# A softmax-attention block and two feed-forward layers on one core: later w_in products, and a table that shifts 32 operations in a list scheduler

## The chip, the cores and the metric

The kernel runs on one core of one Trainium2 chip. Five engines of the core share the work: TensorE (PE in the profile, with PEld for its weight loads), VectorE (DVE), ScalarE (ACT), GpSimd (POOL) and SyncE (SP), which here does nothing but issue DMAs. The metric is the device time of one execution in microseconds, of which the median over three runs is given.

## The reference, cut to what matters

Eight heads in each of four batches attend to 32 state rows, and the state rows attend back to the 512 tokens; the results go through two feed-forward layers of 2304 tokens each.

```python
scores = x @ state.T / 8;   a  = softmax(scores);   xread = a @ state       # per head: 512 x 32 scores
scores2 = state @ x.T / 8;  a2 = softmax(scores2);  sread = a2 @ x
x = concat(xread, sread)                       # (2304 tokens, 512)
h = x @ w_in                                   # moe: 512 -> 2048
g = where(h >= 1, h, where(h <= -1, 0, (h + 1) ** 2 / 4))
x = g @ w_out                                  # 2048 -> 512
a, b = x @ w_a, x @ w_b                        # moe2: 512 -> 1536
out = (a * b) @ w_out2                         # 1536 -> 512
```

Everything is float32. The weights arrive as 64-bit words and are turned to float32 on the chip.

## The kernel before, in words

**Precision by parts.** A large product is made in three passes. Each operand is split into a high part (ACT copies it into the fp32r type, `hi_of`, line 346) and a low part (DVE subtracts the high part from the operand, `tt`, line 356); PE then adds up high x high, high x low and low x high (`mms`, line 371). So before nearly every PE step there stands one ACT instruction and one DVE instruction.

**Phase one** is the attention with the first layer's first product, `h`. The tokens of a batch are one block `j` (0 to 3), the hidden features 16 groups `f`; one step `t = 16 j + f` makes the unit `h_mm(j, f)`: six matmuls of 512 columns into one of four PSUM banks. Then `gate` (lines 779, 788 and 793) applies the activation: ACT, then ACT or POOL, then DVE, which frees the bank, then a store to the scratch tensor `g_d`.

What `h_mm(j, f)` reads was folded beforehand. The product `xread @ w_in` is never made from `xread`: `w_state(j, n)` (line 660, called by `phase_one`) multiplies the state of block j with four groups of `w_in` (f = 4n to 4n + 3) into a PSUM pair named `upper`; ACT and DVE split that into the buffer `wsum[n]`; then `h_mm` multiplies `wsum` with the softmax `att`. There is one `wsum[n]`, so `w_state(j + 1, n)` may only overwrite it when `h_mm(j, 4n + 3)` is done, and must be done before `h_mm(j + 1, 4n)`. For the first groups of block 0 it is made in pieces of 128, 128 and 256 columns.

Beside it run: `w_in(f, 2)`, which loads two groups of weights and turns them to float32 in three steps, `copy` (ACT, DVE or POOL: line 421 or 423), `byte` (ACT, line 346) and `join` (DVE, line 434); the scores and softmax of the next block (`b_qk`, line 526, `b_soft`, lines 543 to 569); the state's own attention of each block (`s_soft`, lines 695 to 726, `s_tr`, line 743, `s_read`, line 758), through a PSUM pair named `lower`; and the conversion of `w_out` (`conv`, then `v_early`, `v_upper`, `v_rest`: sums of quarters in line 904, on DVE or POOL, and splits in 356).

**The later phases** are `g @ w_out` (`b_steps`) in three chunks of tokens, and the second layer (`ab_run`, `o_run`). They are made with seven block products in place of eight, whose sums and differences of quarters DVE makes (line 904), each followed by a split (ACT 346, DVE 356) that the next twelve matmuls wait for. `late` puts the second layer's weights (`w_sums`, `w_put`) into the end of `b_steps`.

**What sets the order.** Nothing is issued where it is written. Each operation is recorded by `Flow.op` with its engines, an assumed cost, what it reads and writes. `Flow.order` then lists all 2344 operations: for each it works out a latest start `late` backwards from the end, and steps through assumed time, giving each engine the ready operation with the smallest `late`. PE operations keep the order in which they were recorded, save those marked `loose`, which may be put in wherever PE would wait. Where an operation may run on several engines, the listing picks one. The result is a fixed order of instructions on each engine and in SP's DMA queue; on the chip each engine runs its list in order and waits at semaphores.

Of the kernel before, what the change touches and what calls it, by code (L numbers as in the profile page):

```python
# [14 lines left out]
AX = mybir.AxisListType  # L15
PSUM = bass.MemoryType.PSUM
DRAM = bass.MemoryType.DRAM


class Flow:  # L20
# [13 lines left out]
    def __init__(self):  # L34
        self.ops = []
        self.last = {}
        self.readers = {}
        self.loose = set()
        self.gate = None
        self.hold = None  # L40
        self.row = None
        self.rush = 0.0
        self.port = set()
        self.hurry = {}

    def op(self, engs, emit, rd=(), wr=(), size=0, loose=False, port=False):
        i = len(self.ops)
# [37 lines left out]
    def order(self):  # L85
# [24 lines left out]
        for i in range(n - 1, -1, -1):  # L110
# [5 lines left out]
            if i in ideal:  # L116
                late[i] = min(late[i], ideal[i])
        late = [x - self.hurry[i] for i, x in enumerate(late)]
        free = dict.fromkeys(self.LAT, 0.0)
        ready = {e: [] for e in free}  # L120
        left = [len(d) for _, _, d, _ in ops]
# [13 lines left out]
        for _ in range(n):  # L135
# [39 lines left out]
                fin[i] = wire + self.DMA_LAT  # L175
            for s in after[i]:
                left[s] -= 1
                when[s] = max(when[s], free[e] if (e,) == (*ops[s][0],) and not ops[i][3] else fin[i])
                if not left[s]:
                    offer(s)  # L180
            self.ops[i] = (*ops[i][:4], e)
# [5 lines left out]
def attention_then_two_mlps(  # L187
# [458 lines left out]
    def w_state(*args):  # L646
        for f in w_steps(*args):
            f()

    def w_steps(b, n, f0=0, f1=4):  # L650
# [4 lines left out]
        def emit(e):  # L655
            for j in range(4):
# [14 lines left out]
                emit,  # L671
                regs(*st, win.sub(2048 * n + 512 * f0, 512 * (f1 - f0))),
                [bank(b) for b in ab],
                loose=b == 0 and n > 0,
            )
        ]
        for q in [range(2)] if WIDE and cols == 4 * P else [range(1), range(1, 2)]:
# [654 lines left out]
    def phase_one():  # L1332
# [39 lines left out]
        for b, (soft, tr, read, after) in enumerate(TIMES):  # L1372
            PLAN.setdefault(soft, []).append((s_soft, b))
            PLAN.setdefault(tr, []).append((s_tr, b))
            PLAN.setdefault(read, []).append((s_read, b))
            if b < 3:
                if b:
                    PLAN.setdefault(16 * b - 5, []).append((st_load, b + 1))
                PLAN[soft].append((lambda b: (a_load(2 * b), a_load(2 * b + 1)), b + 1))
                PLAN.setdefault(after, []).extend([(b_qk, b + 1), (b_soft, b + 1)])  # L1380
        nv = 0
        for t in range(4 * F1):
            j, f = divmod(t, F1)
# [4 lines left out]
            h_mm(j, f, (1,) if t < HALVES else range(2))  # L1388
            for g in (v1, v2)[t] if t < 2 else ():
                g()  # L1390
            if j < 3 and f % 4 == 3:
                w_state(j + 1, f // 4)
            for what, b in PLAN.get(t, ()):
                flow.hold = units[HOLD] if b < 1 else None
                flow.rush = RUSH[b]
# [97 lines left out]
    for t0 in pairs:  # L1493
        o_run(t0, t0 == pairs[-1])

    order = flow.order()
    with tc.manual_schedule():
        nc.vector.memset(half, 0.5)
# [79 lines left out]
```

## Time and profile before

| | |
|---|---|
| median of 3 runs | 720.42 us (719.61 to 723.85) |
| the profiled execution | 719.44 us, its span 717.3 us |
| PE busy | 699.2 us, 97% |
| DVE, ACT, POOL busy | 559.3, 424.8, 97.3 us |

The span is the time between the first and the last instruction; 2.1 us lie around it. A PE matmul counts as busy also where it runs at half the clock; the granted clock is in the windows' column PEclk (1.00 is 2.4 GHz).

### The profile page before, as it was taken

To read this page: it belongs to the slowest core of one execution; us is meant where nothing else is said; L and a number is where in the kernel's file an instruction comes from. 1 tells how busy PE (TensorE), PEld (TensorE's weight loads), DVE (VectorE), ACT (ScalarE), POOL (GpSimd) and SP (SyncE) were. 2 spreads that over 40 slices of the span, in tenths; PEclk is the share of its full clock that TensorE was granted. 3 is DMA by queue.
4 is the path that set the end of the run, shared out by engine and by line. 5 is a ranking of instruction groups with operands and counts; after the bars stand their busy time and mean duration, and the time that the engine had idled before them with its cause. 6 is when DMAs were issued, how large, how long until landed. Compare 5 with 4: busy or idle time off the path is not lost.

```text
span 717.3 us, 12235 instructions
## 1 busy us (share of the span) xinstructions
PE 699.2 (97%) x4818; PEld 655.4 (91%) x4818; DVE 559.3 (78%) x701; ACT 424.8 (59%) x625; POOL 97.3 (14%) x72
## 2 busy tenths in 40 slices
PE   7799999999999999999999999999999999999997
PEld 5456667989899999999999999999999999999997
DVE  6888879988998687899899786655636798987760
ACT  4787989797544446666566675655425535544440
POOL 3346555573100000000000000000000000000000
PEclk9999999999999999999999999999999999999999
DMA  9867967497466157143425767454541248454201
GB/s 346 357 214 245 357 236 272 149 349 250 147 200 242 35 162 219 50 141 138 133 99 203 226 203 243 157 167 135 183 163 42 87 150 279 127 188 136 87 30 44
DMA packets 75449, 128.92 MB, mean 180 GB/s; under 512 B 5632, under 2 KB 51200, under 8 KB 75392
## 3 DMA queue, kind: packets, MB, share of 16 engines
q1 hardware_dynamic: 75392, 128.15, 53.1%
q8 instruction: 37, 0.61, 0.4%
q14 instruction: 20, 0.16, 0.1%
HBM read 84.87 MB, written 43.25 MB: 179 GB/s over the span
## 4 chain that ended last, share of the span: by engine, by line
PE 82%; DVE 7%; DMA 5%; ACT 2%; issue 2%; POOL 1%; SPq 0%; DVEq 0%; POOLq 0%; ACTq 0%
PE bank L371 76%; DMA f<-in_w_dram 2%; PE bank L829 2%; DVE rh L356 2%; DMA p_d<-f 1%; DMA f<-p_d 1%; PE upper L660 1%; DVE r L356 1%; PE lower L758 1%; PE bank L853 1%; ACT f L346 1%; DVE fs L434 1%; DVE fs L549 1%; DVE fs L793 1%; ACT rh L346 0%
## 5 line engine op out<-in xcount | busy, mean ns | idle before, releaser
L371 PE MATMUL bank<-rh,r 128*128 128x352 f32 (+2 forms) x1398 | 223.5, 316 | 2.6 <-DVE rh L356 2.1
L371 PEld LDWEIGHTS bank<-rh,r 128*128 128x128 f32 x1398 | 215.8, 189 | 4.6 <-DVE rh L356 3.0
L371 PE MATMUL bank<-r,r 128*128 128x368 f32 (+1 forms) x960 | 156.1, 315 | 0.0
L346 ACT ACTIVATE f<-bank 128x368 f32<-128x368 f32 (+3 forms) x183 | 82.4, 453 | 119.3 <-PE bank L371 118.3
L371 PEld LDWEIGHTS bank<-r,r 128*128 128x128 f32 x960 | 147.9, 188 | 0.0
L346 ACT ACTIVATE rh<-f 128x736 fp32r<-128x736 f32 (+5 forms) x120 | 100.7, 846 | 77.7 <-PE bank L371 61.3
L356 DVE TENSOR_TENSOR rh<-f,rh 128x736 fp32r<-128x736 f32 (+5 forms) x120 | 120.2, 1014 | 26.1 <-ACT rh L346 25.6
L356 DVE TENSOR_TENSOR f<-bank,f 128x368 f32<-128x368 f32 (+2 forms) x168 | 85.6, 516 | 69.0 <-PE bank L371 64.0
L371 PE MATMUL bank<-r 128*128 128x512 f32 (+1 forms) x582 | 122.1, 362 | 2.8 <-ACT r L346 1.1
L371 PEld LDWEIGHTS bank<-r 128*128 128x128 f32 x582 | 95.5, 191 | 28.5 <-issue 5.1
L346 ACT ACTIVATE r<-f 128x768 fp32r<-128x768 f32 (+6 forms) x85 | 80.0, 952 | 40.8 <-PE bank L371 17.6
L356 DVE TENSOR_TENSOR r<-f,r 128x768 fp32r<-128x768 f32 (+6 forms) x85 | 91.9, 1090 | 15.7 <-ACT r L346 15.6
L371 PE MATMUL bank<-rh 128*128 128x352 f32 (+2 forms) x564 | 93.3, 318 | 0.5 <-DVE f L356 0.5
L904 DVE TENSOR_TENSOR f<-f 128x256 f32<-128x256 f32 (+7 forms) x108 | 85.8, 811 | 6.3 <-DMA f<-p_d 5.2
L371 PEld LDWEIGHTS bank<-rh 128*128 128x128 f32 x564 | 88.4, 189 | 1.4 <-issue 0.7
L371 PE MATMUL bank<-r,rh 128*128 128x368 f32 (+1 forms) x480 | 80.3, 315 | 0.0
L371 PEld LDWEIGHTS bank<-r,rh 128*128 128x128 f32 x480 | 74.3, 188 | 0.0
L346 ACT ACTIVATE f<-f 128x1024 fp8e5<-128x1024 f32 (+1 forms) x43 | 47.8, 1120 | 2.2 <-POOL f L423 2.0
L421 ACT ACTIVATE f<-f 128x512 fp8e5<-128x512 fp8e5 (+1 forms) x29 | 29.5, 1018 | 24.5 <-DMA f<-in_w_dram 18.4
L434 DVE SCALAR_TENSOR_TENSOR f<-f 128x1024 uint32<-128x1024 uint32 (+1 forms) x34 | 34.9, 1027 | 5.9 <-ACT f L346 5.8
L779 ACT ACTIVATE f<-bank,half 128x512 f32<-128x512 f32 x40 | 27.1, 686 | 8.1 <-PE bank L371 4.4
L793 DVE SCALAR_TENSOR_TENSOR f<-f,bank 128x512 f32<-128x512 f32 x40 | 26.3, 675 | 6.6 <-POOL f L788 4.0
(65 smaller groups left out, 425.9 us busy)
## 6 DMA issues: line engine op xcount, KB each, us to landing
f<-in_w_dram SPq DMA_DIRECT2D x25, 1024.0 KB, 6.2
f<-g_d SPq DMA_DIRECT2D x36, 368.0 KB, 5.5
f<-p_d SPq DMA_DIRECT2D x17, 768.0 KB, 5.0
g_d<-f SPq DMA_DIRECT2D x40, 256.0 KB, 4.3
f<-in_w_dram SPq DMA_DIRECT2D x18, 512.0 KB, 3.9
p_d<-f SPq DMA_DIRECT2D x48, 184.0 KB, 2.1
g_d<-fs SPq DMA_DIRECT2D x28, 256.0 KB, 3.6
f<-g_d SPq DMA_DIRECT2D x16, 352.0 KB, 4.5
```

What stands on the lines that cost most here:

```text
L346: lambda e: nc.scalar.activation(dst(), src(), func, **{k: (v() if callable(v) else v) for k, v in kws.items()}),
L356: op({"DVE": t_tt(n)}, lambda e: nc.vector.tensor_tensor(dst(), a(), b(), alu), rd, wr, port=port)
L371: nc.tensor.matmul(o, w, x, start=first and k == 0, stop=last and k == n - 1, skip_group_check=onto)
L421: nc.scalar.activation(to(), of(), AF.Copy, saturate=False)
L434: lambda e: nc.vector.scalar_tensor_tensor(out(U32), words_of(1, U32)(), 5, z(U32), ALU.logical_shift_right, ALU.bitwise_or),
L549: op({"DVE": 1.25}, lambda e: nc.vector.transpose(t1(), wide["lower"]), both, regs(t1))
L660: nc.tensor.matmul(banks[ab[q]][o : o + NS, :cols].rearrange("p (f x) -> p f x", x=P), st[q]()[64 * h : 64 * h + 64, NS * j : NS * j + NS] ...
L758: nc.tensor.matmul(banks[4][64 * e2 : 64 * e2 + 64, o : o + NS], xn()[:, c * 256 + p * 128 + e2 * 64 : c * 256 + p * 128 + (e2 + 1) * 64], ...
L779: lambda e: nc.scalar.activation(g(), h(), AF.Relu, bias=half[:, 0:1], scale=0.5),
L793: lambda e: nc.vector.scalar_tensor_tensor(g(), g(), 1.0, h(), ALU.min, ALU.max),
L829: nc.tensor.matmul(banks[b][:, P * i : P * i + P], w[:, P * c : P * c + P], xs()[:, P * c : P * c + P], start=c == 0, stop=c == 3,)
L904: lambda e: eng(e).tensor_tensor(dst(), a(), b(), alu),
```

## The change

Three things. `w_state` of blocks 1 to 3 is marked `loose` too, and called some four steps later (`AHEAD` gives, for a step t, the pair of block and n). `Flow.order` takes a table `NUDGE`: for an operation's number in the recording, an amount taken off its latest start (positive: earlier in the choice, negative: later), and for two of them an engine that it may not use. And an operation keeps the scheduler's rule for operations with one engine, as it was recorded, where the table takes an engine away.

```diff
+NUDGE = {
+    64: (119,), 65: (2433,), 72: (638,), 78: (-4.5,), 79: (20.5, "POOL"), 90: (-9.5,), 92: (658.5,), 100: (78,),
...
+    1278: (9.5,),
+}
@@ Flow.order
+        single = [len(e) == 1 for e, _, _, _ in ops]
+        for i, (x, *off) in self.nudge.items():
+            late[i] -= x
+            ops[i] = ({e: t for e, t in ops[i][0].items() if e not in off}, *ops[i][1:])
...
-                when[s] = max(when[s], free[e] if (e,) == (*ops[s][0],) and not ops[i][3] else fin[i])
+                when[s] = max(when[s], free[e] if single[s] and e in ops[s][0] and not ops[i][3] else fin[i])
@@ w_steps
-                loose=b == 0 and n > 0,
+                loose=b > 0 or n > 0,
@@ phase_one
+        AHEAD = {7: [(1, 0)], 11: [(1, 1)], 15: [(1, 2)], 19: [(1, 3)], 22: [(2, 0)], 26: [(2, 1)], 30: [(2, 2)], 34: [(2, 3)], 38: [(3, 0)], 42: [(3, 1)], 45: [(3, 2)], 47: [(3, 3)]}
...
-            if j < 3 and f % 4 == 3:
-                w_state(j + 1, f // 4)
+            for b, n in AHEAD.get(t, ()):
+                w_state(b, n)
...
+    flow.nudge = NUDGE
     order = flow.order()
```

Line numbers of the changed kernel are 14 higher in what follows (660 becomes 674).

**The order at three places.** First, PE in the first 45 us. `bank0` to `bank3` (L371) are units of `h_mm` of block 0, in the order of f from 1 on; `upper` (L660) are `w_state` products, `lower` L743 the transposes of `s_tr`, L758 `s_read`. Before:

```order
L371 MATMUL bank1_68<-r0_65 128x512 x6
L660 MATMUL upper_88<-fs_92 32x256 x8
L660 MATMUL upper_88<-fs_92 32x512 x8
L371 MATMUL bank2_69<-r0_65 128x512 x6
L371 MATMUL bank3_70<-r0_65 128x512 x6
L660 MATMUL upper_88<-fs_92 32x512 x8
L371 MATMUL bank0_67<-r0_65 128x512 x6
L743 MATMUL lower_87<-ident_64,fs_92 128x128 x4
L371 MATMUL bank1_68<-r0_65 128x512 x6
L743 MATMUL lower_87<-ident_64,fs_92 128x128 x4
```

And now:

```order
L385 MATMUL bank1_68<-r0_65 128x512 x6
L674 MATMUL upper_88<-fs_92 32x256 x8
L385 MATMUL bank2_69<-r0_65 128x512 x6
L674 MATMUL upper_88<-fs_92 32x512 x8
L385 MATMUL bank3_70<-r0_65 128x512 x6
L757 MATMUL lower_87<-ident_64,fs_92 128x128 x4
L385 MATMUL bank0_67<-r0_65 128x512 x6
L757 MATMUL lower_87<-ident_64,fs_92 128x128 x4
L674 MATMUL upper_88<-fs_92 32x512 x8
L385 MATMUL bank1_68<-r0_65 128x512 x6
L772 MATMUL lower_87<-fs_92 64x32 x32
L674 MATMUL upper_88<-fs_92 32x512 x8
```

The unit f = 2 now stands ahead of the product for f = 4 to 7; block 1's first product, which followed the unit f = 3, now comes after f = 5 (last row), and the product for f = 8 to 11, which followed f = 7, now follows f = 4.

On DVE in the same place (L434 joins weights, L423 is a `copy`, L356 `128x128` and `128x256` are the low parts that the units f = 1 and f = 2 wait for, L695 `s_soft`'s maximum) there stood:

```order
L434 SCALAR_TENSOR_TENSOR fs_92<-f0_66 128x1024
L434 SCALAR_TENSOR_TENSOR fs_92<-f0_66 128x512
L423 COPY f0_66<-f0_66 128x1024
L356 TENSOR_TENSOR r0_65<-upper_88,r0_65 128x128 x2
L695 TENSOR_REDUCE fs_92<-lower_87 128x2
L434 SCALAR_TENSOR_TENSOR fs_92<-f0_66 128x1024 x2
L356 TENSOR_TENSOR r0_65<-upper_88,r0_65 128x256 x2
```

Now:

```order
L448 SCALAR_TENSOR_TENSOR fs_92<-f0_66 128x512
L448 SCALAR_TENSOR_TENSOR fs_92<-f0_66 128x1024
L709 TENSOR_REDUCE fs_92<-lower_87 128x2
L370 TENSOR_TENSOR r0_65<-upper_88,r0_65 128x128 x2
L807 SCALAR_TENSOR_TENSOR f0_66<-f0_66,bank0_67 128x512
L715 TENSOR_SCALAR fs_92<-fs_92 128x2
L448 SCALAR_TENSOR_TENSOR fs_92<-f0_66 128x1024
L437 COPY f0_66<-f0_66 128x1024
L370 TENSOR_TENSOR r0_65<-upper_88,r0_65 128x256 x2
```

The narrow join is first, the first copy has gone to POOL (another stands in its place further down), the maximum has moved ahead, and one of the two wide joins has moved behind the 256-wide low parts.

Second, POOL at the end of phase one. L904 are sums of quarters of `w_out`, L788 squares of `gate`; the last row of before runs beside the splits of `b_steps`' second and third products.

```order
L904 TENSOR_TENSOR f0_66<-f0_66 128x4x256 x2
L788 TENSOR_TENSOR f0_66<-f0_66 128x512 x3
L904 TENSOR_TENSOR f0_66<-f0_66 128x4x256
L788 TENSOR_TENSOR f0_66<-f0_66 128x512
L904 TENSOR_TENSOR f0_66<-f0_66 128x4x256
L788 TENSOR_TENSOR f0_66<-f0_66 128x512 x5
L904 TENSOR_TENSOR f0_66<-f0_66 128x4x256 x2
```

Now:

```order
L918 TENSOR_TENSOR f0_66<-f0_66 128x4x256
L557 TENSOR_TENSOR fs_92<-fs_92 128x1024
L918 TENSOR_TENSOR f0_66<-f0_66 128x4x256
L437 COPY f0_66<-f0_66 128x1024
L918 TENSOR_TENSOR f0_66<-f0_66 128x4x256
L802 TENSOR_TENSOR f0_66<-f0_66 128x512
L918 TENSOR_TENSOR f0_66<-f0_66 128x4x256 x4
L802 TENSOR_TENSOR f0_66<-f0_66 128x512 x4
L918 TENSOR_TENSOR f0_66<-f0_66 128x4x256
L802 TENSOR_TENSOR f0_66<-f0_66 128x512 x4
```

There are eight sums on POOL in place of six (DVE has the two fewer), four of them stand in a row, and four squares follow the last one.

Third, DVE in the last chunk of `b_steps`, where `w_put` splits the second layer's first weights (`128x512` and `128x1280`) between the splits that PE waits for (`128x2x352`); L356 with `bank` adds a finished PSUM bank and frees it.

```order
L356 TENSOR_TENSOR rh_1271<-f1_1275,rh_1271 128x2x352
L356 TENSOR_TENSOR rh_1271<-f1_1275,rh_1271 128x512
L356 TENSOR_TENSOR rh_1271<-f1_1275,rh_1271 128x1280
L356 TENSOR_TENSOR rh_1271<-f1_1275,rh_1271 128x2x352 x3
L356 TENSOR_TENSOR f0_66<-bank5_1256,f0_66 128x352
L904 TENSOR_TENSOR f0_66<-f0_66 128x256
L356 TENSOR_TENSOR f0_66<-bank4_1255,f0_66 128x352
```

Now:

```order
L370 TENSOR_TENSOR rh_1274<-f1_1278,rh_1274 128x2x352
L370 TENSOR_TENSOR f0_66<-bank4_1258,f0_66 128x352
L370 TENSOR_TENSOR rh_1274<-f1_1278,rh_1274 128x512
L370 TENSOR_TENSOR f0_66<-bank5_1259,f0_66 128x352
L370 TENSOR_TENSOR rh_1274<-f1_1278,rh_1274 128x2x352 x2
L370 TENSOR_TENSOR rh_1274<-f1_1278,rh_1274 128x1280
L370 TENSOR_TENSOR rh_1274<-f1_1278,rh_1274 128x2x352
```

The 1280-wide low part stands behind two more of the splits, and the two bank additions ahead of them.

## Rows read from the trace of the kernel before

**Rows 1.** The page: span, and busy time of each engine.

```profile
span 717.3 us, 12235 instructions
PE 699.2 (97%) x4818; PEld 655.4 (91%) x4818; DVE 559.3 (78%) x701; ACT 424.8 (59%) x625; POOL 97.3 (14%) x72
```

**Rows 2.** Windows, by stage: length, busy us of each engine, clock, DMA share.

```profile
18.00:27.00 9.00, 4.41 (x51) 2.20 (x59) 8.63 (x12) 6.93 (x11) 2.53 (x2) 1.00 1.03 409
27.00:32.00 5.00, 5.00 (x27) 3.33 (x23) 4.13 (x6) 4.14 (x7) 2.12 (x3) 0.66 1.02 406
32.00:60.00 28.00, 25.94 (x238) 16.52 (x238) 24.69 (x29) 22.64 (x29) 14.68 (x11) 1.00 0.63 206
60.00:128.00 68.00, 67.05 (x590) 46.30 (x588) 56.55 (x72) 59.45 (x91) 41.68 (x32) 1.00 0.78 278
128.00:176.00 48.00, 48.00 (x302) 44.13 (x295) 42.44 (x42) 39.91 (x55) 24.74 (x14) 1.00 0.75 255
176.00:190.00 14.00, 12.49 (x73) 11.78 (x72) 13.86 (x11) 8.51 (x9) 5.38 (x2) 1.00 0.27 83
295.00:330.00 35.00, 33.94 (x209) 33.34 (x209) 32.22 (x37) 20.94 (x30) 0.00 (x0) 1.00 0.42 138
330.00:718.00 388.00, 383.47 (x2627) 382.79 (x2625) 279.93 (x386) 199.78 (x307) 0.00 (x0) 1.00 0.45 144
```

**Rows 3.** Waits of PE: for whom, us in total, times, longest.

```profile
PE upper L660 <- DVE r L356: 4.1, 3, 2.5
```

**Rows 4.** Timeline of PE, 20 to 62: start, us, tile, shape, count [idle before <-releaser].

```profile
20.64 0.45 PE L660 MATMUL upper<-fs 64*32 64x128 f32 x16 [1.33 <-DVE fs L434]
...
26.87 1.13 PE L660 MATMUL upper<-fs 64*32 64x512 f32 x16 [2.46 <-DVE r L356]
...
54.36 1.09 PE L660 MATMUL upper<-fs 64*32 64x512 f32 x16 [1.26 <-DVE r L356]
55.39 5.78 PE L371 MATMUL bank<-r 128*128 128x512 f32 x24
```

**Rows 5.** Timeline of DVE, 18 to 27.

```profile
18.75 1.83 DVE L434 SCALAR_TENSOR_TENSOR fs<-f 128x1024 uint32<-128x1024 uint32 x2 [0.33 <-ACT f L346]
20.62 1.78 DVE L423 COPY f<-f 128x1024 uint8<-128x1024 uint8 x1
...
22.69 1.21 DVE L695 TENSOR_REDUCE fs<-lower 128x2 f32<-128x1024 f32 x1
...
26.07 0.74 DVE L356 TENSOR_TENSOR r<-upper,r 128x256 fp32r<-128x256 f32 x2
```

**Rows 6.** Timeline of ACT: two byte conversions.

```profile
21.81 2.58 ACT L346 ACTIVATE f<-f 128x1024 fp8e5<-128x1024 f32 x2 [0.17 <-POOL f L423]
```

**Rows 7.** Windows: the stretch at half clock.

```profile
27.80:31.20 3.40, 3.40 (x16) 2.60 (x9) 2.53 (x3) 3.40 (x7) 0.93 (x1) 0.50 1.03 411
```

**Rows 8.** Timeline of PE, 60 to 128: the two waits.

```profile
88.45 4.37 PE L371 MATMUL bank<-r 128*128 128x512 f32 x18 [0.57 <-DVE fs L793]
...
119.39 2.06 PE L758 MATMUL lower<-fs 128*64 128x32 f32 x64 [0.38 <-ACT fs L346]
```

**Rows 9.** Timeline of DVE and POOL, 139 to 186: quarter sums, splits beside them.

```profile
139.52 1.23 DVE L904 TENSOR_TENSOR f<-f 128x1024 f32<-128x1024 f32 x1
...
176.27 5.46 POOL L904 TENSOR_TENSOR f<-f 128x1024 f32<-128x1024 f32 x2 [7.80 <-DVE r L356]
177.45 5.06 DVE L356 TENSOR_TENSOR rh<-f,rh 128x736 fp32r<-128x736 f32 x2
184.64 0.91 DVE L356 TENSOR_TENSOR rh<-f,rh 128x736 fp32r<-128x736 f32 x1
```

**Rows 10.** Timeline of DVE and PE, 294 to 330: six splits, two PE waits.

```profile
294.30 5.30 DVE L356 TENSOR_TENSOR rh<-f,rh 128x704 fp32r<-128x704 f32 x6
...
298.04 29.11 PE L371 MATMUL bank<-rh,r 128*128 128x352 f32 x179 [0.60 <-DVE rh L356]
327.61 2.65 PE L371 MATMUL bank<-rh 128*128 128x352 f32 x15 [0.46 <-DVE f L356]
```

More of the change, by code (lines that the diff above doesn't have):

```diff
@@ L17 @@
 DRAM = bass.MemoryType.DRAM
+NUDGE = {
+    64: (119,), 65: (2433,), 72: (638,), 78: (-4.5,), 79: (20.5, "POOL"), 90: (-9.5,), 92: (658.5,), 100: (78,),
+    109: (-9,), 138: (69,), 163: (-32,), 196: (-9,), 219: (-12.5,), 304: (7.5,), 328: (6, "ACT"), 1010: (33,),
+    1011: (30.5,), 1092: (10,), 1094: (-1.5,), 1096: (10,), 1103: (5.5,), 1138: (-5.5,), 1170: (10,),
+    1172: (191.5,), 1182: (-1,), 1201: (-5,), 1208: (29.5,), 1211: (27,), 1213: (10.5,), 1217: (8,), 1235: (-4.5,),
+    1278: (9.5,),
+}
 class Flow:
@@ L44, in __init__ @@
         self.hurry = {}
+        self.nudge = {}
     def op(self, engs, emit, rd=(), wr=(), size=0, loose=False, port=False):
```

## The prediction

> **What bounds the kernel now.** I read the page first: PE is busy 699.2 of 717.3 us [rows 1]. What PE has to multiply is not changed by one matmul, so only two things can be won: the time in which PE stands still, 18.1 us, and the time in which its clock is down. Next, the windows by stage, to see where that lies [rows 2]: 18 to 27 us leaves PE idle for 4.59 us, 32 to 60 for 2.06, 60 to 128 for 0.95, 176 to 190 for 1.51, 295 to 330 for 1.06. The stretch 128 to 176 leaves nothing, and the last 388 us only 4.53, of which the end of the last store is most. Of the first 18 us the lists of instructions are the same in both kernels. Last, who ends the waits: the longest is the `w_state` product into `upper`, 4.1 us in three waits for a subtraction on DVE [rows 3], and DVE is busy 8.63 of 9 us from 18 to 27 and 24.69 of 28 from 32 to 60. So up to 60 us the order of DVE's list sets the time, and PE pays for each instruction that stands ahead of the one it waits for. Behind 60 us PE itself is the bound, with four short waits in it.
>
> **Head, 18 to 32 us.** (a) The 1024-wide join waits 0.33 us for ACT and stands ahead of the 512-wide one, and a copy of 1.78 follows [rows 5] (1.83 for both joins, so by width about 1.2 and 0.6); the product for the unit f = 1 waits 1.33 us for the narrow join [rows 4]. With the narrow one first, that product can start when PE comes to it, at 20.64 - 1.33 = 19.3. The low parts that the unit f = 1 needs stood behind two joins and the copy, so at about 18.75 + 1.83 + 1.78 = 22.3; now they stand behind the two joins (from 18.4, no wait) and the maximum of 1.21, so at 18.4 + 1.83 + 1.21 = 21.4: about 0.8 earlier. (b) The 256-wide low parts for f = 2 start at 26.07 [rows 5], because ACT had two byte conversions of 2.58 us ahead of their high parts [rows 6]; these start earlier, since the copy before them now runs on POOL. On DVE there are, from 21.4, the two small low parts (0.5, from 0.74 for twice the width), a gate as wide as the narrow join (0.6), a wide join (1.2) and a copy of 1.78 or less: 25.3. (c) PE idles 2.46 us and then makes the product for f = 4 to 7 first [rows 4]. In the new order the unit f = 2 goes into that idle time: four units take 5.78 [rows 4], one 1.4. The product needs the second wide join, which now stands behind the 256-wide low parts: 25.3 + 0.74 + 1.2 = 27.2, against 26.87. So at this point PE is 1.4 - 0.3 = 1.1 us ahead; bounds 0 and 1.5.
>
> (d) From 27.8 to 31.2 the granted clock is 0.50, that is 1.2 GHz, with PE busy throughout [rows 7]: 3.4 us at half speed lose 1.7. It fell behind the stage in which PE was busy 4.41 of 9 us [rows 2], and every later window shows 1.00. Where PE does the unit f = 2 earlier, it is busier ahead of 27.8, about 5.8 of 9. The rows show one fall and no near miss, so they can't say whether that is enough. I take half, 0.85; bounds 0 and 1.7. The Trainium skill (TensorE: Matmul & The Clock Gate, section "What's actually happening") calls the slow clock the default, which activity releases; the trace agrees as far as 0.50 follows the emptiest stage, and by that rule the fuller PE keeps its clock, which would make the sum 0.85 larger.
>
> **32 to 60 us: 2.06 idle, of which 1.26 is one wait** at 54.36 for DVE [rows 2, 4]. The deferred products each take 1.09 of PE [rows 4], one ACT instruction and a subtraction of about 1.2 on DVE with them; up to the unit f = 12 there is one fewer than before. That is not work saved, it returns between 60 and 128, but there DVE has 11.4 us of slack [rows 2]. Against it stands the product for f = 8 to 11, moved from behind f = 7 to behind f = 4. It needs the join of f = 10, which on DVE follows the low part of the product made at 27.2 (1.1 on PE, a high part as long as one conversion, 1.3 [rows 6], a low part as long as a sum of that width, 1.2 [rows 9]: 30.8) and another copy: 30.8 + 1.8 or less + 1.2 = 32.5 to 33.8. PE is there after two more units and a transpose, near 32. PE's list is strict, so all units stand behind that wait; I take 1.0. Net 2.06 - 1.0 = 1.05; bounds -1.0 (DVE as late as before, and the new wait) and 2.06. Head together: 1.1 + 0.85 + 1.05 = **3.0**, between -1.0 and 5.3.
>
> **60 to 128: 0.95 idle** [rows 2]. The wait of 0.38 for ACT before `s_read` of the last block [rows 8] goes, because a unit and a product (1.4 + 1.1 us) now stand between its transposes and it. The wait of 0.57 for a gate on DVE stays: gate, transposition, gate stand as before. I take **0.4**. Above, 0.95; below, -1.7, three new waits like that one, since ACT is busy 59.45 of 68 us.
>
> **176 to 190: 1.51 idle** [rows 2]. Two splits of 736 columns take 5.06 us together beside two sums on POOL of 5.46, while one alone takes 0.91 [rows 9]: 3.2 us lost on DVE, and PE's two waits follow. Both sums now run earlier, so the splits get back to 0.9 and both waits go. But the sums run somewhere else, beside other two-operand instructions of DVE, in a stage where PE has waited for nothing yet. I take **1.0**; above 1.5, below see the first rival.
>
> **295 to 330: 1.06 idle** [rows 2]. The split at whose end PE starts at 298.04 stood behind a 1280-wide subtraction. Six of them in a row take 5.30 [rows 10], four of 704 columns, one of 512 and the widest; by width (4608 columns) these are about 0.8, 0.6 and 1.5. That one now comes two splits later, and two bank additions of about 0.5 come ahead: 0.5 less, and a small sum that also went behind gives 0.4 more. That makes 0.9, against 0.60 of idle time. The bank addition that ends the second wait (0.46 idle) now comes ahead of a split instead of behind it, 0.8 earlier. I take **0.9**; bounds 0 and 1.06. Past 330 us, little can be won (4.53, mostly the end), and the few changes there I cost at nothing; PE at 383.47 of 388 covers them, and if that cover fails they cost a wait of half a us each.
>
> **Sum.** 3.0 + 0.4 + 1.0 + 0.9 = 5.3. The profiled execution takes 719.44, 0.98 under the median of 720.42; against it 714.1, and as a median 720.4 - 5.3 = **715.1**.
>
> **Rivals.** *The sums on POOL hold DVE up (slower).* The row says that a split beside a POOL sum takes 2.5 us in place of 0.9 [rows 9]. POOL gets eight sums for six, four in one row, all ahead of 176. DVE has 48 - 42.44 = 5.56 us of slack from 128 to 176 [rows 2], and 2.46 more without its own two sums of 1.23 [rows 9]: 8.0. Into this stage come four more POOL sums. If each holds up one DVE instruction by 1.6, that is 6.4, and PE notices nothing. If each holds up two, it is 12.8, 4.8 over the slack, and the units of block 3 wait for their banks. The point is 2.0 us of delay for each sum. Together with a head at its lower bound of -1.0, nothing from 60 to 128 and the two later gains (1.5 and 0.9): -1.0 - 4.8 + 1.5 + 0.9 = -3.4, or 723.8. For it: DVE at 42.44 of 48; against: many of DVE's instructions there read PSUM. The Trainium skill (GPSIMD Engine Reference, section "Key points") says that GpSimd shares its SBUF interfaces with VectorE, with contention where DVE has two SBUF inputs; the trace agrees with 2.5 against 0.91. By that rule alone every such DVE instruction under a sum pays, as in the case with two.
>
> *The waits only change place.* DVE remains as full as it was up to 60 us, so a product that PE meets earlier waits there instead, and the clock falls again: head 0.2, nothing to 128, 1.0 and 0.9 behind: 2.1, or 718.3. This also holds if the list does on the chip what it did before, because its order rests on assumed durations (a DVE instruction beside POOL is taken there as at most doubled, and the row says 2.8 times). For it: DVE at 24.69 of 28 and the DMA share above 1.0 from 18 to 32 [rows 2], so the weights cannot come sooner.
>
> *Every wait goes and the clock stays up*: 5.3 + 0.95 + 1.5 + 1.06 = 8.8, or 711.6. For it: the lists put work of PE into each of the gaps named.
>
> **Chances.** The forecast's case (gains of 3.2 to 7.2) 0.58; every wait goes 0.16; waits change place 0.19; the slower one 0.07. One per cent is 7.2 us, about what a measurement of this kernel can tell from no change; faster by more than that needs nearly all that stands still behind 18 us, so 0.17; slower by more than 1% (over 727.6) would need a second loss of the first rival's size, 0.03; within, 0.80. The range: from 710.6, the best case with 1.0 for the spread of the runs, to 720.6, which holds the waits that change place with a loss of 2.3 more and leaves out the slower rival.
>
> **What would show it.** In the new profile: PE's `upper` products no longer lead the table of waits, and the 2.46 us before the product of f = 4 to 7 shrink to under 1; the wait moves to the product of f = 8 to 11, near 33 us. The window near 28 to 31 shows 1.00 or 0.50, which decides 1.7 us. Splits of 736 columns take 0.9 throughout 176 to 190 with PE at 14 of 14; in 128 to 176 PE stays within 0.5 of full. At 295 to 330 PE misses under 0.3. The prediction is wrong if DVE's two-operand instructions at 130 to 165 take 2.5 us in number and PE waits for gates there, or if ACT, fuller than any other engine but PE from 60 to 128, makes new waits of its own.

## The result, and the profile after

The changed kernel takes **711.81 us** (median of 4 runs, 711.13 to 711.93) against 720.36 (719.61 to 723.85) in the same comparison: a ratio of 0.987, interval 0.984 to 0.990. The gain is 8.55 us where 5.3 were forecast; it lies inside the range, but beyond the forecast's own case (3.2 to 7.2) and just beyond one per cent, which had got a chance of 0.17.

The profiled execution took 711.84 us, its span 710.1. The page, span and busy times, answering [rows 1]:

```profile
span 710.1 us, 12246 instructions
PE 697.3 (98%) x4818; PEld 653.9 (92%) x4818; DVE 556.5 (78%) x701; ACT 421.1 (59%) x622; POOL 105.3 (15%) x75
```

PE stands still for 710.1 - 697.3 = 12.8 us, where it was 18.1: 5.3 us less. The windows by stage, as in [rows 2], with one more for 190 to 295:

```profile
18.00:27.00 9.00, 6.01 (x53) 2.70 (x60) 7.91 (x14) 7.84 (x14) 4.19 (x3) 0.89 1.02 409
27.00:32.00 5.00, 4.90 (x32) 2.60 (x16) 3.58 (x3) 3.62 (x5) 1.56 (x2) 0.85 1.02 409
32.00:60.00 28.00, 27.01 (x245) 17.34 (x244) 26.76 (x34) 24.94 (x38) 13.75 (x11) 1.00 0.68 236
60.00:128.00 68.00, 67.55 (x603) 49.20 (x602) 58.13 (x70) 58.49 (x86) 48.96 (x35) 1.00 0.83 289
128.00:176.00 48.00, 48.00 (x290) 43.24 (x290) 43.76 (x41) 38.65 (x52) 30.53 (x16) 1.00 0.70 236
176.00:190.00 14.00, 14.00 (x85) 14.00 (x84) 12.98 (x12) 6.59 (x9) 0.00 (x0) 1.00 0.51 160
190.00:295.00 105.00, 104.59 (x627) 103.83 (x626) 85.16 (x97) 54.75 (x76) 0.00 (x0) 1.00 0.49 161
295.00:330.00 35.00, 35.00 (x218) 34.79 (x217) 33.08 (x38) 22.09 (x32) 0.00 (x0) 1.00 0.43 135
```

Idle time of PE by stage, before and after: 18 to 32 us 4.59 and 3.09, 32 to 60 2.06 and 0.99, 60 to 128 0.95 and 0.45, 176 to 190 1.51 and 0, 190 to 295 0 and 0.41, 295 to 330 1.06 and 0. In the table of waits, the products into `upper` no longer lead [rows 3]; units of `h_mm` that wait for their weights do:

```profile
PE bank L385 <- ACT r L360: 2.0, 3, 0.8
PE bank L385 <- DVE r L370: 1.6, 2, 0.9
...
PE upper L674 <- DVE fs L448: 0.4, 1, 0.4
```

PE's timeline shows where they are, beside [rows 4]:

```profile
18.97 0.73 PE L385 MATMUL bank<-r 128*128 128x512 f32 x2 [0.56 <-ACT r L360]
20.46 1.19 PE L385 MATMUL bank<-r 128*128 128x512 f32 x4 [0.76 <-DVE r L370]
...
23.04 0.73 PE L385 MATMUL bank<-r 128*128 128x512 f32 x2 [0.79 <-ACT r L360]
24.64 1.75 PE L385 MATMUL bank<-r 128*128 128x512 f32 x4 [0.87 <-DVE r L370]
26.32 1.96 PE L674 MATMUL upper<-fs 64*32 64x512 f32 x16
...
33.09 0.66 PE L757 MATMUL lower<-ident,fs 128*128 128x128 f32 x4 [0.99 <-ACT fs L740]
33.67 1.09 PE L674 MATMUL upper<-fs 64*32 64x512 f32 x16
```

The wait of 2.46 us ahead of the product for f = 4 to 7 is gone; the units f = 1 and f = 2 wait four times for under 0.9 us. A new wait near 33 us is there as foreseen, 0.99 us, but one step earlier, at the transposes and for ACT instead of a join on DVE. The product takes 1.96 us in place of 1.13 because the clock fell again, as in [rows 7]:

```profile
25.10:28.40 3.30, 3.30 (x21) 0.89 (x20) 3.14 (x4) 1.33 (x3) 1.35 (x1) 0.50 1.03 413
```

DVE and POOL around the sums of quarters, beside [rows 9]:

```profile
137.37 11.46 POOL L918 TENSOR_TENSOR f<-f 128x1024 f32<-128x1024 f32 x4
138.05 2.79 DVE L370 TENSOR_TENSOR r<-f,r 128x1024 fp32r<-128x1024 f32 x1
141.36 2.83 DVE L370 TENSOR_TENSOR rh<-f,rh 128x1024 fp32r<-128x1024 f32 x1
146.51 3.11 DVE L370 TENSOR_TENSOR rh<-f,rh 128x736 fp32r<-128x736 f32 x1
...
174.33 1.93 DVE L370 TENSOR_TENSOR rh<-f,rh 128x736 fp32r<-128x736 f32 x2
```

Three splits are slow beside the four sums in a row, but PE is busy 48.00 of 48 us there; the two splits of 736 columns that took 5.06 beside late sums, the ninth and tenth of their kind, now take 1.93. And PE at the third place, beside [rows 10]:

```profile
274.02 7.84 PE L385 MATMUL bank<-rh,r 128*128 128x352 f32 x47 [0.41 <-DVE rh L370]
281.71 7.83 PE L385 MATMUL bank<-rh 128*128 128x352 f32 x48
289.37 31.11 PE L385 MATMUL bank<-rh,r 128*128 128x352 f32 x192
```

Both waits of [rows 10] are gone; one of 0.41 us has come at 274.

**How far ahead, and since when.** The same matmul starts in the two traces at 16.52 and 15.24 us (first unit of `h_mm`), 142.37 and 138.24 (first of block 3), 190.60 and 184.35, 283.52 and 277.84, 299.93 and 293.24, 327.61 and 320.32, and the last at 713.72 and 706.50. The lead is 1.28, 4.13, 6.25, 5.68, 6.69, 7.29 and 7.22 us. The first 1.28 are there before the lists differ. They come from the first stretch; PE's timeline of before, and then of after:

```profile
1.36 5.06 PE L853 MATMUL bank<-ident 128*128 128x128 f32 x22 [1.36 <-POOL ident masks.py:199]
```

```profile
1.36 4.25 PE L867 MATMUL bank<-ident 128*128 128x128 f32 x22 [1.36 <-POOL ident masks.py:199]
```

The same 22 matmuls take 0.81 us less, because the clock rose from 0.50 to 1.00 earlier in that execution, at 4.58 us for 7.32. In the 14 traces of this case the first unit, up to which PE's list is the same in all, starts between 15.08 and 16.60 us. So 1.28 us of the traced gain is chance; 5.94 come behind it.

### The profile page after: what moved, and what is told of

The parts are those of the page before. It is cut to its first block, busy times and chain, and to the rows that moved or that the text cites. A ratio compares the mean times of both kernels' runs of the same rounds, so it can differ in the third digit from the quotient of the medians.

```text
span 710.1 us, 12246 instructions
## 1 busy us (share of the span) xinstructions
PE 697.3 (98%) x4818; PEld 653.9 (92%) x4818; DVE 556.5 (78%) x701; ACT 421.1 (59%) x622; POOL 105.3 (15%) x75
## 4 chain that ended last, share of the span: by engine, by line
PE 89%; DMA 4%; DVE 3%; ACT 2%; issue 1%; POOL 0%; DVEq 0%; POOLq 0%; ACTq 0%
PE bank L385 82%; PE bank L843 2%; PE upper L674 2%; DMA f<-in_w_dram 2%; DMA g_d<-fs 1%; PE lower L772 1%; DMA f<-g_d 1%; ACT f L360 1%; PE bank L867 1%; DVE f L918 1%; DVE rh L370 1%; DVE r L370 1%; DMA f<-x_d 0%; PE lower L540 0%; PE lower L757 0%
## 5 line engine op out<-in xcount | busy, mean ns | idle before, releaser
L385 PE MATMUL bank<-rh,r 128*128 128x352 f32 (+2 forms) x1398 | 222.4, 316 | 0.9 <-ACT f L360 0.5
L385 PEld LDWEIGHTS bank<-rh,r 128*128 128x128 f32 x1398 | 215.9, 189 | 1.7 <-DVE rh L370 0.7
L385 PE MATMUL bank<-r,r 128*128 128x368 f32 (+1 forms) x960 | 156.2, 315 | 0.0
L385 PEld LDWEIGHTS bank<-r,r 128*128 128x128 f32 x960 | 147.8, 188 | 0.1
L370 DVE TENSOR_TENSOR f<-bank,f 128x368 f32<-128x368 f32 (+2 forms) x168 | 85.8, 517 | 72.3 <-PE bank L385 68.0
L370 DVE TENSOR_TENSOR rh<-f,rh 128x736 fp32r<-128x736 f32 (+5 forms) x120 | 119.2, 1002 | 25.5 <-ACT rh L360 25.0
L385 PE MATMUL bank<-r 128*128 128x512 f32 (+1 forms) x582 | 121.1, 360 | 4.5 <-ACT r L360 2.0
L385 PEld LDWEIGHTS bank<-r 128*128 128x128 f32 x582 | 94.7, 190 | 30.0 <-issue 8.4
L370 DVE TENSOR_TENSOR r<-f,r 128x768 fp32r<-128x768 f32 (+6 forms) x85 | 94.3, 1122 | 15.6 <-ACT r L360 15.6
L385 PE MATMUL bank<-rh 128*128 128x352 f32 (+2 forms) x564 | 93.5, 318 | 0.1
L385 PEld LDWEIGHTS bank<-rh 128*128 128x128 f32 x564 | 88.4, 189 | 1.2 <-DVE f L370 0.6
L918 DVE TENSOR_TENSOR f<-f 128x256 f32<-128x256 f32 (+6 forms) x106 | 83.3, 804 | 6.1 <-DMA f<-p_d 5.0
L385 PE MATMUL bank<-r,rh 128*128 128x368 f32 (+1 forms) x480 | 80.3, 315 | 0.0
L385 PEld LDWEIGHTS bank<-r,rh 128*128 128x128 f32 x480 | 74.3, 188 | 0.0
```

What stands on the lines that cost most here:

```text
L370: op({"DVE": t_tt(n)}, lambda e: nc.vector.tensor_tensor(dst(), a(), b(), alu), rd, wr, port=port)
L385: nc.tensor.matmul(o, w, x, start=first and k == 0, stop=last and k == n - 1, skip_group_check=onto)
L918: lambda e: eng(e).tensor_tensor(dst(), a(), b(), alu),
```

## The experiments

**Splices.** In the first four kernels the order is a fixed list, made of the new list up to one unit and of the old one behind it, or the other way round; what runs is the same. With the list in the file, line numbers are some 130 higher (L674 becomes L801, L385 L512, L370 L497).

```diff
-    order = flow.order()
+    order = ORDER
+    for i, e in enumerate(ENGINE):
+        flow.ops[i] = (*flow.ops[i][:4], names[e])
```

*New up to the first unit of block 1 (60 us), then old.*

> The lists of the changed kernel up to the first unit of block 1 (about 60 us), those of the kernel before from there on. Theory A (each group of moves takes away the wait beside it, and the gains add up): 1.9 us faster than before, as the profiles' lead at equal work says (3.1 at that unit, less 1.3 that was there before the lists differ), so 718.5; the PE waits at 176 to 190 and 295 to 330 are there as before. Rival G (the lead of the head is given back, since DVE and ACT are nearly full behind it): under 0.5 us. Rival S (the lead is where the clock rises in that execution, not the lists): between 0 and 1.3, without a wait less in 18 to 60.

Measured: 720.00 us (before beside it 720.91), ratio 0.9991, 0.9970 to 1.0011: nothing that can be told from no change. PE's timeline at the seam:

```profile
60.40 1.96 PE L801 MATMUL upper<-fs 64*32 64x512 f32 x16 [2.08 <-DVE r L497]
62.29 5.07 PE L512 MATMUL bank<-r 128*128 128x512 f32 x18
```

PE comes to the first product of the old list early and waits 2.08 us for DVE; then the clock falls, and the product takes 1.96 us in place of 1.09, the 18 matmuls 5.07 in place of 4.37. In this trace the lead of the head is gone: less the start of the execution, the product begins as late as before.

*New up to the first unit of block 3 (about 138 us), then old.*

> The new lists up to the first unit of block 3 (about 128 us in the profile before), the old ones from there. Theory A: 2.9 us faster than before (lead 4.1 at that unit in the profiles, less 1.3), 717.5. Rival G: under 1. Rival S: as with the new lists to 60 us.

Measured: 715.02 us, ratio 0.9927, 0.9900 to 0.9955: 5.9 us are won by then, twice the 2.9 of Theory A. PE's two waits behind the late sums are still in its trace, 0.75 us each, at 181 and 184 us.

*New up to the fifth split of the third product group (about 200 us), then old.*

> The new lists up to the fifth split of the third product group (about 200 us), the old ones from there. Theory A: 4.9 us faster than before, since the 1.8 of waits at 184 and 188 go too: 715.5; PE then waits at 297 and 327 as before (1.06). Rival: the lead of the earlier part is lost where the sums on POOL hold DVE up, and this kernel is no faster than the one that is new to 128 us.

Measured: 712.60 us, ratio 0.9896, 0.9868 to 0.9924: another 2.4 us, 8.3 in all, where Theory A had 4.9; the two waits of 0.75 are gone, and those of 0.60 and 0.46 at 293 and 323 us are there as before the change. The rest of the list, with that place, brings the remaining 0.8 to the new kernel's 711.81; the forecast for it was 0.9. The two times come from different comparisons, though: by the gains, each over its own kernel before (720.91 and 720.36), it is 0.2, by the traces, less the start, 1.2.

*Old up to the first unit of block 1, then new.*

> The old lists up to the first unit of block 1, the new ones from there. Theory A: what the whole change gains less the part of the head: 8.5 - 1.9 = 6.6 by the medians, 4.1 by the profiles; so 714 to 716, with the head's waits (2.46 at 26.9, 1.26 at 54.4) as before. Rival G or S: as fast as the changed kernel within 1 us, since the head's moves bring nothing.

Measured: 718.46 us, ratio 0.9968, 0.9949 to 0.9987. Both theories missed: the whole change behind 60 us is worth only 2.5 us with the old head. PE's timeline at the seam shows the mirror image of the first splice, a wait for ACT:

```profile
63.37 1.27 PE L884 MATMUL lower<-ident,fs 128*128 128x128 f32 x8 [1.86 <-ACT fs L867]
```

So head and middle do not add up: 0.9 (not clear of nothing) for the one and 2.5 for all that follows it, but 8.6 together. In both traces PE waits at the seam for an engine whose list behind it does not have its work that early. A caution goes with all four: part of what a seam costs is the seam's own, and no run separates the two.

**The old order traced once more**, as a fixed list, nothing changed:

> The order of the kernel before, written out as a fixed list: nothing is changed in what runs. The question is what a second execution of it shows on the clock. Theory K: the one fall of the clock in the profiled execution is the least that this order has (the timed executions of the kernel before have mean granted clocks of 0.990 to 0.998, most 0.993, and one fall of 3.4 us at half speed lowers the mean by 0.0024), so this trace shows two to four falls, all ahead of 100 us, and each shows PE's work of that stretch taking longer. Rival: one fall again, at about 28 us, and the lower means come from somewhere else. Time 719 to 721 by both.

Measured: 720.73 us, span 718.9, against 717.3 in the first trace. The theory that this trace would show more falls of the clock was wrong: one fall again, at the same place, with a mean clock of 0.998. Where the lower means of the timed executions come from, neither trace shows. But there are two waits that the first trace does not have:

```profile
280.26 7.84 PE L512 MATMUL bank<-rh,r 128*128 128x352 f32 x47 [0.28 <-DVE rh L497]
...
383.76 0.94 PE L512 MATMUL bank<-r,rh 128*128 128x368 f32 x4 [0.51 <-DVE rh L497]
```

By its time the first trace was one of the old order's better executions; by the clock neither trace is a usual one.

**The late sums alone.** Old lists; the last split of `v_early` and the last two sums of POOL moved ahead of the squares and splits that they stood behind:

```diff
 after the second low part of v_upper
+    split (v_early, fourth): high part ACT, low part DVE
+    v_sum (v_early, sixth): POOL
+    v_sum (v_upper, second): POOL
```

> The old order, with only the last two sums of POOL and the split ahead of them moved to before the two splits of 736 columns. Theory S (POOL beside DVE is what PE waits for from 176 to 190 us): the splits take 0.9 us each, PE is busy 14 of 14 us there, and the time falls by 1.5 to 2.1 us, to about 718.8. Rival G (given back): DVE pays the same time for these sums earlier, or the next product waits for its weights, and the gain is under 0.5 us, about 720.5.

Measured: 725.31 us against 721.22, ratio 1.0067, 1.0043 to 1.0090, slower by 4.1. POOL's and PE's timelines, and the window:

```profile
160.97 5.44 POOL L1045 TENSOR_TENSOR f<-f 128x1024 f32<-128x1024 f32 x2 [3.72 <-DVE r L497]
166.38 4.48 POOL L929 TENSOR_TENSOR f<-f 128x512 f32<-128x512 f32 x3
169.64 2.93 PE L512 MATMUL bank<-r 128*128 128x512 f32 x6 [3.75 <-DVE f L934]
...
176.00:190.00 14.00, 14.00 (x81) 13.54 (x81) 10.01 (x11) 10.67 (x13) 0.00 (x0) 1.00 0.44 133
```

Theory S was right about 176 to 190 us: no sum there, PE at 14.00 of 14. It did not see the price: the squares now queue behind the sums on POOL, the gates that need them come late, and a unit of block 3 waits 3.75 us for its bank, after which the clock falls (six matmuls take 2.93 us for 1.53). This is the end of the prediction's slower rival, units of block 3 that wait for their banks, by another way. In the new lists four sums run at 137 us and one alone at 156, and PE is busy 48.00 of 48 us there.

**The two halves of the change.** First the freed and later products without the table (`flow.nudge = NUDGE` left out):

```diff
-    flow.nudge = NUDGE
```

> The freed products and their later recording, without the table of 32 moves. In its lists the product for f = 4 to 7 still stands ahead of the unit f = 2, and the last sums of POOL still come singly, up to the splits of 736 columns. Theory A (the place of each step makes the gain): the wait of 2.5 us near 26 us and the slow splits stay, and the time is 719.5 to 722. Rival L (to have the products free of program order makes most of the gain): 714 to 716.

Measured: 720.69 us against 721.22, ratio 0.9976, 0.9953 to 0.9999. The wait of 2.47 us ahead of the product for f = 4 to 7 stands as before, and the one near 88 us, 0.57 before [rows 8], has grown to 3.03:

```profile
25.55 1.74 PE L674 MATMUL upper<-fs 64*32 64x512 f32 x16 [2.47 <-DVE r L370]
...
88.02 8.58 PE L385 MATMUL bank<-r 128*128 128x512 f32 x24 [3.03 <-DVE fs L807]
```

The table alone, its numbers carried over to the same operations:

```diff
-                loose=b > 0 or n > 0,
+                loose=b == 0 and n > 0,
...
-            for b, n in AHEAD.get(t, ()):
-                w_state(b, n)
+            if j < 3 and f % 4 == 3:
+                w_state(j + 1, f // 4)
```

> The table of 32 moves alone, its numbers carried over to the steps that they mean, with the products recorded and bound as before. Theory A (table and freed products only work together, since the numbers shift steps against one another): the product for f = 4 to 7 stands ahead of the unit f = 2 again, and the time is 719 to 723. Rival T (the table alone makes the gain): 711.5 to 714.

Measured: 724.04 us, ratio 1.0039, 1.0016 to 1.0062: slower, with a wait of 4.49 us at 58 us. Neither half makes the gain.

**One swap on PE.** New lists, with the product for f = 4 to 7 put back ahead of the unit f = 2:

```diff
 PE
-    h_mm(0, 2)
     w_state(0, 1)
+    h_mm(0, 2)
     h_mm(0, 3)
```

> The new order with one swap on PE alone: the product for f = 4 to 7 ahead of the unit f = 2, as before the change. Theory W (this place is worth what the prediction says, and the wait lowers the clock as well): a wait of 2 us or more stands before that product again, the next units run at 0.50, PE is 1.1 us behind at 32 us or more, and the time is 713 to 714.5. Rival D (VectorE's list sets the pace up to 60 us, whatever PE does first): the loss is caught up by 60 us and the time is within 0.4 of the new order, 711.5 to 712.3.

Measured: 713.55 us (712.68 to 714.47), ratio 0.9904, 0.9881 to 0.9927; the new kernel is at 711.81, so the swap costs 1.7 (1.6 by the gains). PE's timeline:

```profile
26.02 1.92 PE L801 MATMUL upper<-fs 64*32 64x512 f32 x16 [3.26 <-DVE fs L575]
```

Theory W fits by the medians. In the traces the unit f = 4 starts 1.36 us later than in the new kernel, 0.51 of it from the start of the execution: 0.85 us for the place, where the prediction had 1.1. By the end of that trace, which is the fastest of the four, only 0.13 are left of it: the new kernel's trace has waits of 0.45 and 0.41 us at 97 and 274 us, where PE, coming later, finds its work ready. The medians hold one thing more: all four executions with the swap have a mean clock of 0.998, one fall, where three of the new kernel's four have 1.000. So part of the 1.7 is the clock.

**Keeping the clock up.** Multiplications of the identity into the PSUM pair `lower`, in PE's idle places of the old lists (18 and 36 matmuls in the trace, twice the time that the expectation gives, since each appears as two):

```diff
+    warm 9             # ahead of w_state(0, 0), f = 1
     w_state(0, 0)
...
+    warm 18            # ahead of w_state(0, 1)
     w_state(0, 1)
```

> The old order, with extra multiplications of the identity, whose result nobody reads, in two of PE's idle places: 9 (1.1 us) ahead of the product for f = 1 and 18 (2.3 us) ahead of the product for f = 4 to 7. Nothing else moves. Theory K (the falls of the clock are a large part of what the old order loses): the clock stays at 1.00 behind 27 us, the mean granted clock of the timed executions rises from 0.993 to 0.997 or more, and the time falls by 1.5 to 3 us, to 718 to 719.5. Rival D (VectorE sets the pace there, and the falls lie elsewhere): the time stays at 720.5 to 721.5.

Measured: 720.86 us against 720.54, ratio 1.0003, 0.9990 to 1.0016. All ten executions have a mean clock of 0.999 or 1.000, where those of before lie at 0.992 to 0.995. PE's timeline:

```profile
24.25 4.29 PE L1677 MATMUL lower<-ident 128*128 128x128 f32 x36
28.46 1.09 PE L804 MATMUL upper<-fs 64*32 64x512 f32 x16
...
33.49 1.66 PE L515 MATMUL bank<-r 128*128 128x512 f32 x6
...
54.45 1.09 PE L804 MATMUL upper<-fs 64*32 64x512 f32 x16 [1.27 <-DVE r L498]
```

The fill is too long by 1.6 us (the product starts at 28.46, before at 26.87), the clock that stays up gives that back by 33.49 (33.41 before), and at 54 us PE waits for DVE as it did, 1.27 and 1.26 [rows 4]. Theory K's gain of 1.5 to 3 us did not come. But the run is a weaker test than it was meant to be, since the fill put PE back by what the kept clock then returned, 1.5 us for one fall. As an estimate: if all of the fill's 1.6 us reaches the end, the falls of the clock are worth 1.6 us within -1.2 and +0.7, the interval of the ratio, so 0.4 to 2.3 us of the old order's time.

This trace also shows a wait that differs between executions. From 75 to 83 us its engines run within 0.06 us of the first trace of before, and SP issued the loads of weights at the same times (74.49 and 74.53 us). But the weights that POOL copies landed later, and all that stands behind the copy came later. Before, and then here:

```profile
83.33 1.37 POOL L423 COPY f<-f 128x1024 uint8<-128x1024 uint8 x1 [1.96 <-DMA f<-in_w_dram]
```

```profile
84.74 1.37 POOL L567 COPY f<-f 128x1024 uint8<-128x1024 uint8 x1 [3.32 <-DMA f<-in_w_dram]
86.03 1.92 POOL L687 TENSOR_TENSOR fs<-fs 128x1024 f32<-128x1024 f32 x1
...
87.98 1.25 DVE L707 STREAM_TRANSPOSE fs<-fs 128x1024 f32<-128x1024 f32 x1 [2.87 <-POOL fs L687]
...
89.86 4.37 PE L515 MATMUL bank<-r 128*128 128x512 f32 x18 [1.93 <-DVE fs L937]
```

The gate on DVE stands behind that transposition, so PE waits 1.93 us where it was 0.57 [rows 8]. The 3.03 us of the kernel without the table lie in the same place, behind a copy that waited 4.21 us for its weights. None of the traces with the new lists there has this wait.

The same in the new lists, four places:

```diff
     w_state(0, 0)      # f = 1
+    warm 4
     h_mm(0, 1), high parts
+    warm 5
     h_mm(0, 1), the rest
     w_state(0, 0)      # f = 2, 3
+    warm 5
     h_mm(0, 2), high parts
+    warm 6
     h_mm(0, 2), the rest
```

> The new order, with such extra multiplications in its four idle places from 18 to 25 us, 4, 5, 5 and 6 of them (0.5 to 0.75 us each). Theory K: no fall of the clock behind 25 us; since only some executions of the new order have one, and the shortest without one is 1.1 us ahead of the one with it, the gain is 0 to 0.6: 711.2 to 711.8. Rival: the extra work keeps PE from its own when that comes ready, 0.3 to 1 us slower, 712 to 713.

Measured: 715.70 us, ratio 0.9934, 0.9912 to 0.9956: 3.9 slower than the new kernel. The fill is twice too long here too, and two of its four wait themselves, 1.67 and 1.49 us, since DVE and ACT use the same PSUM pair; the first, for DVE's maximum over it:

```profile
21.18 1.16 PE L1677 MATMUL lower<-ident 128*128 128x128 f32 x8 [1.67 <-DVE fs L839]
```

For the clock the run says nothing. For the head it says something: PE is put back by 3.1 us at the unit f = 4 (4.19 less 1.10 from the start), and 2.3 of it are left at the end of the trace, 3.9 by the medians. Here most of the head's time reaches the end, unlike in the trace of the swap.

**The sums off POOL.** New lists, two of POOL's eight sums back on DVE at their place in the order:

```diff
-    v_sum (v_early, fourth), v_sum (v_upper, first): POOL
+    v_sum (v_early, fourth), v_sum (v_upper, first): DVE
```

> The new order, with the two sums of 1024 columns that it moves to POOL put back on VectorE. Theory S (POOL's sums hold VectorE's splits up, but the stage from 128 to 176 us has the slack for it): the splits beside them get back from 2.8 to 3.1 us towards 0.9 to 1.3, PE stays at 48 of 48 us, and the time is that of the new order, 711.4 to 712.3. Rival P (the sums must be off VectorE): its list is longer by 2.5 us, gates come late, and the time is 713 to 714.5.

Measured: 711.64 us (710.71 to 713.11), ratio 0.9879, 0.9855 to 0.9904, the same as the new kernel. DVE's timeline, then the window:

```profile
137.10 2.79 DVE L497 TENSOR_TENSOR r<-f,r 128x1024 fp32r<-128x1024 f32 x1
...
147.83 0.91 DVE L497 TENSOR_TENSOR rh<-f,rh 128x736 fp32r<-128x736 f32 x1
...
128.00:176.00 48.00, 48.00 (x287) 43.23 (x286) 43.89 (x43) 38.48 (x52) 23.61 (x13) 1.00 0.69 230
```

The split that had taken 3.11 us takes 0.91, the two beside the sums that stay on POOL stay slow, and PE notices neither. Which engine makes these two sums doesn't matter here.

No experiment gave a version that beats the new kernel by more than the spread.

## Why the prediction was right, and where it was not

**PE's idle time: right by stage, in places by other waits than foreseen.** Steps (a) to (c) put 1.1 us on 18 to 32; it lost 1.50. The new wait at 33 us was taken as 1.0, which left 1.05 for 32 to 60; it is 0.99, which leaves 1.07. The number is partly luck: the prediction meant a wait for the join of f = 10, and in this trace the transposes ahead of that product wait for ACT. Where the clock stayed up, PE waits for both (below). For 60 to 128 it was 0.4; it is 0.50, and this is luck too: the wait of 0.38 before the last `s_read` went as foreseen, but the 0.57 for the gate, which was to stay, went as well, and 0.45 came before another block's `s_read`. For 176 to 190, 1.0; the trace shows the full 1.51, and moving the sums alone emptied that stage of waits. For 295 to 330, 0.9; the full 1.06. Against these stands the wait at 274, 0.41, which was not foreseen. In sum 5.3 us of idle time went. The forecast of 5.3 held 0.85 for the clock, so its waits alone were 4.45, 0.85 too few: in the traced execution two misses of the same size cancel.

**The clock (d): nothing in the traced execution, but it counts in the others.** In the trace it fell again, for as long as before, although PE was busy 5.52 of the 9 us ahead of the fall (16.1 to 25.1) where it had been 4.41 (18.8 to 27.8). Yet three of the new kernel's four timed executions have a mean clock of 1.000, so no fall, and of the 57 timed executions of the kernel before whose clock is known none has more than 0.998 and most have 0.993. The rule of the Trainium skill that the prediction weighed (TensorE: Matmul & The Clock Gate, section "What's actually happening"), that activity releases the fast clock, spoke for a gain; the traced execution does not bear it out, since PE was fuller and the clock fell all the same, and the other three agree with it.

The price of a fall can be read from kernels whose lists are the new ones on every engine up to 136 us. The sums put back on DVE, and the splice to block 3, have no fall in their traces; PE at the product for f = 8 to 11 there, one after the other:

```profile
33.27 1.09 PE L801 MATMUL upper<-fs 64*32 64x512 f32 x16 [0.36 <-DVE fs L575]
```

```profile
33.07 1.09 PE L801 MATMUL upper<-fs 64*32 64x512 f32 x16 [0.53 <-DVE fs L575]
```

Counted from the first unit of `h_mm`, which starts at 16.32 and 15.69 us, they are 1.48 and 1.05 us ahead of the new kernel's trace (33.67, from 15.24), and keep it to 95 us. The splice to 200 us, whose clock fell, is level with it (0.08 behind). So a fall there costs 1.0 to 1.5 us of the 1.7 that 3.4 us at half speed lose, because PE, earlier without it, waits for ACT (0.88 us in both) and for the join. The 0.85 was taken blind, as half of 1.7; an execution without the fall gains more.

**The sum: too small by 3.25 us, and where they are.** The traced executions differ by 719.44 - 711.84 = 7.60: 5.3 of idle time, 1.9 of busy time and 0.4 outside the spans (2.14 and 1.74 us). Of the 1.9, 1.28 are the start of the execution, chance; the other 0.6 stay unexplained. To 8.55 there are 0.95 more, and here the sum was mis-sized: the prediction took the old kernel's 0.98 between trace and median as a constant and carried it to the new one, whose trace lies on its median. What is in the 0.98 stays open; the runs show two candidates. One is waits that come in some executions of the old order only: 0.28 and 0.51 us in its second trace, and at 88 us 1.93 in place of 0.57 where the weights landed 1.4 us later. The other is the clock: both traces of the old order have 0.998, but 55 of the 57 timed executions 0.995 or less. A mean of 0.993 over 719 us is about 10 us at half speed, three times the one fall of the traces, and none of its traces shows such an execution. The runs with the clock kept up bound all falls together at 0.4 to 2.3 us, by the estimate above.

In 61 timed runs the kernel before took 718.25 to 726.17 us, the new one 711.13 to 711.93 in 4. A spread over four runs is narrower by itself: the four runs of before beside the new kernel spread by 4.2 us, the new ones by 0.8. The kernels with the new list up to 128 us or further and nothing added spread by 0.8 to 2.4 over four runs each, the others by 1.2 to 5.9 over their first four. So the new order looks steadier, which the prediction did not see; the wait for late weights is one thing that it loses, and whether that is all is not settled.

**The rivals.** *Sums on POOL hold DVE up*: the slow splits are there, 2.79 to 3.11 us beside four sums in a row, but the stage has the slack, and taking two of the sums off POOL changes nothing. The rival also counted too many: from 128 to 176 us run six sums where four ran before, two more and not four. The Trainium skill (GPSIMD Engine Reference, section "Key points") has POOL and DVE share their way to SBUF; the three slow splits agree, and the time says that it costs nothing there. What did cost time is the queue on POOL: with the sums ahead of the squares in the old lists the kernel was 4.1 us slower. *The waits only change place*: for the head alone this is what happened (720.00 with the old list behind it); with the new lists behind it, it did not. *Every wait goes and the clock stays up*, 711.6, gave nearly the measured time, and half of its condition holds: the clock stays up in three of four executions, but four waits are left in the head, 2.98 us in the trace, so that the sum comes out is partly luck.

**By stage, the medians disagree with the traces in one point.** The splices put 5.9 us on the time to 138 us, 2.4 on 138 to 200 and 0.8 on the rest; the traces, less the start, 2.85, 2.1 and 1.0. The difference is in the first part. The trace of the splice to block 3 itself ends 3.0 us ahead of the old order's first trace, less the start (713.72 - 709.86, less 0.83), so it agrees with the traces: the rest of the 5.9 lies in how much longer the old order's timed executions are than its trace, and there its cause is open as above.

## What to carry to other kernels

In a kernel with fixed lists a gain at one place can be lost at the next, where the lists of the other engines are not as far: look at the next place where PE would come early, and at whom it would wait for there. Where a sum or copy is moved off a busy stretch, look at what queues behind it in its new place, on its own engine, before looking at contention. And one trace is one execution: before a forecast takes its distance to the median as a constant, a second trace of the same program is worth having, and the mean clock of the timed executions shows whether the trace is a usual one.

## What the runs showed of the hardware

The clock rises at another time in each execution, and the start of the work moves with it: in the 14 traces the first unit starts between 15.08 us, where the clock rose at 4.24, and 16.60, where it rose at 7.47. Behind 50 us, the falls of the clock in these traces each come with a long wait of PE (2.08, 3.03, 3.75 and 4.49 us) and add to it: after 3.03 us of waiting, 24 matmuls took 8.58 us where 24 take 5.75 at 2.4 GHz; after 3.75 us, six took 2.93 in place of 1.53. The wait of 3.03 us thus cost PE 5.9 in all. After waits of 1.86 and 1.93 us in two other traces the clock stayed up. With the same lists, whether it falls near 26 us differs between executions, and a fall there costs 1.0 to 1.5 us. A load of weights that POOL waits for landed 1.4 us later in one execution than in another (84.74 and 83.33 us), though it was issued at the same time within 0.05 us.
